# Chunk steps once in 1.5 steps, a fifth half block less in four-product form, GpSimd sums in earlier steps

## The chip, the cores and the metric

The kernel runs on one core of a Trainium2 chip. The metric is the device time of one execution, in microseconds; the figure of a version is the median over several executions. The engines are TensorE (PE; its weight loads are shown apart as PEld), VectorE (DVE), ScalarE (ACT), GpSimd (POOL) and SyncE (SP). SP issues most DMAs, ScalarE a few. Each engine works through its own instructions in order and waits where an operand is not ready.

## The reference

Two blocks, one behind the other, in float32 (the weights come as 64-bit words and are converted on the chip):

```python
# q, k, v: (4, 8, 768, 64); gamma: one number per head
for t in range(S):
    state = gamma * state + einsum('bhd,bhe->bhde', k[:, :, t], v[:, :, t])
    y[:, :, t] = scale * einsum('bhd,bhde->bhe', q[:, :, t], state)
x = y.transpose(0, 2, 1, 3).reshape(3072, 512)
h = x @ w_in                 # (512, 2048)
g = h - tanh(h)
out = g @ w_out              # (2048, 512)
```

## The kernel before

**Chunks.** The first block is computed in 24 chunks of 128 tokens. For a chunk, SP loads k, q and v (`load_chunk`, L230), GpSimd scales q and v by powers of gamma (`scale`, L248, the instruction L262), k and q are transposed, TensorE makes 64x64 products of k with v (L325) and of transposed k with transposed q (L331) in `products`, VectorE masks and accumulates the state (`mask` L335, `state` L343), TensorE forms the outputs in `outputs` and `outputs_rest` (both L379), and ScalarE puts them, transposed, into `xT` (`keep_x`, L424). Four chunks fill one `xT` tile of 512 tokens; six such tiles pass through five buffers, some of which the raw weights use at the start and one of which (`fast_x`) holds weight sums later.

From chunk 8 on the transposition is done by DMA (`turn_by_dma`, L294): ScalarE copies k and then q, split into 16-bit halves, into the tile `apart` (L300), its queue writes that to `rows` in DRAM (L303), and SP issues a transposing DMA from `rows` into `kqT` (L305) once the write has landed. There is one `apart` buffer.

**Steps.** The second block works on half blocks of 256 tokens, n = 0 to 11, and on pairs of 128 columns of w_in, m2 = 0 to 7. One (n, m2) is a step; there are 96. A step multiplies x by its two column blocks ("up", into a PSUM tile h, two buffers), forms g = h - tanh(h) on ScalarE and VectorE ("shrink"), and, two or three steps later, multiplies g by w_out ("down"). Steps 0 to 31 interleave n = 0 to 3; from step 32 on n = 4, 5, ... follow with eight steps each. Steps 0 to 7 are in an order written out by hand (L848); the rest come from the loop L925.

From n = 4 on (`FAST_UP`), the up part uses seven products in place of eight (a Strassen scheme; `fast_up`, L756), on sums of weight blocks made by GpSimd (`up_weights`, L736; one of them overwrites a block of w1) and sums of token blocks (`up_tokens`, L746). ScalarE copies the first half's products out (`up_take`, L761), GpSimd adds pairs (`up_pairs`, L766), VectorE adds them in (`up_add`, L771, L773). From n = 5 on (`FAST`), the down part uses seven products of 128x256 (`fast_products`, L647) in place of four of 128x512 (`down`, L510), on sums of w_out blocks (`fast_weights`, L588, each m2 once) and on sums of g (`fast_sums`, L598 to L601, in every step), both on GpSimd; its results are put together by VectorE after the last pair (`fast_end`, L664). The room for these sums is taken over from tiles that the chunks or the weight conversion no longer need.

**Weights.** Steps 9 to 26 also convert one block of 64-bit weights each: ScalarE (L177, L178), VectorE (L186 to L192), GpSimd (L200, L204); SP loads the block three further on, and that load waits until L190 has read the buffer.

**What sets the order around the change.** `with_chunk` (L865) says in which steps a chunk step lies: 9, 11, 13, ... 45, for chunks 5 to 23. The chunk step of chunk ci (`chunk_step`, L899) completes chunk ci, makes the products, mask and state of chunk ci+2, loads chunk ci+4, turns chunk ci+3 and makes the outputs of ci+1. So the transpose that a chunk step begins is needed by the products of the next one. At the end of the step before, GpSimd scales chunk ci+3 (L981). A chunk step stands at the start of its step, ahead of the up part; only in step `FALL` (41) it stands behind the up part's first half. In that step the lag of the down part also grows from two steps to three. `with_sums` (L873) says in which step GpSimd makes which sums.

Of the kernel before, what the change touches and what calls it, by code (L numbers as in the profile page):

```python
# [9 lines left out]
F32 = mybir.dt.float32  # L10
# [6 lines left out]
P = 128  # L17
# [14 lines left out]
def kernel(  # L32
# [27 lines left out]
    NP = H // 2  # L60
    DM = H * D
# [5 lines left out]
    NCH = NT // P  # L67
    BLK = 4
# [10 lines left out]
    xp = ctx.enter_context(tc.tile_pool(name="xp", bufs=NB - 1))  # L79
    tmp = ctx.enter_context(tc.tile_pool(name="tmp", bufs=2))  # L80
    gp = ctx.enter_context(tc.tile_pool(name="gp", bufs=4))
    op = ctx.enter_context(tc.tile_pool(name="op", bufs=4))
# [56 lines left out]
    def load_weights(i):  # L139
        if i >= NW:  # L140
            return
        dst, src = weight_ends(i)
        raw = None
        if w_out.dtype != F32:
            if EARLY <= i < EARLY + 2 * len(rooms):
                raw = rooms[(i - EARLY) // 2][:, (i - EARLY) % 2]
            else:
                raw = stage.tile([P, 2 * BANK], U32, tag="raw", name=f"raw_{i}", bufs=3)
            raws[i] = raw
        if not isinstance(src, list):  # L150
            if raw is None:
                nc.sync.dma_start(out=dst, in_=src)
            else:
                nc.sync.dma_start(out=raw, in_=src.bitcast(U32))
            return
        if raw is not None:
            dst = raw.rearrange("p (c n) -> p c n", c=NC)
        for r, k, w in src:
            nc.sync.dma_start(out=dst[r, k::2], in_=w if raw is None else w.bitcast(U32))  # L159
# [46 lines left out]
    def convert(i):  # L206
        convert_begin(i)
        convert_bits(i)
        convert_end(i, nc.gpsimd)
# [18 lines left out]
    xT = {}  # L228
# [186 lines left out]

    def keep_x(ci):
        n, nj = divmod(ci, BLK)
        if nj == 0:
            xT[n] = xp.tile([P, NP, BLK * P], F32, tag="xT", name=f"xT_{n}")

        half = xT[n][:, :, ts(nj // 2, TH)].rearrange("p (n r) t -> p r n t", r=2)
        y = y_banks[:, ci % 2][:, :: 1 - 2 * (ci % 2)]
        for odd in range(2):
            nc.scalar.copy(out=half[:, :, :, ds(P * odd + D * (nj % 2), D)],  # L424
                           in_=y[:, :, :, odd::2])
# [4 lines left out]
    sums = {}  # L430
# [81 lines left out]

    def add_up(n, m2, j):
        done = 2 * m2 + 2 == NM
        if j == 0 and n not in sums:
            sums[n] = [op.tile([P, 2, DM], F32, tag="sum", name=f"sum_{n}"), set()]
        o, begun = sums[n][0][:, j], sums[n][1]
        if j in begun:
            nc.vector.tensor_tensor(o, o_p[j], o, op=ALU.add)
        elif done and j % 2:  # L520
            nc.vector.tensor_copy(o, o_p[j])
        else:
            nc.scalar.copy(out=o, in_=o_p[j])
        begun.add(j)
        if done:
            nc.sync.dma_start(out=rows_of(n)[:, j], in_=o)

    def rows_of(n):

        return out[ds(n * TH, TH)].rearrange("(p two) c -> p two c", two=2)  # L530
# [17 lines left out]

    FAST = 5
    PAIRS = NM // 2
    t_of = {}

# [27 lines left out]
    def fast_weights(m2):  # L582

        b11, b12, b21, b22 = (w2[:, 2 * m2 + i, ts(c, TH)] for i in range(2) for c in range(2))
        t = {k: next(late_room) for k in (2, 3, 4)}
        t[1] = b12
        for k, x, y in ((3, b22, b12), (1, b12, b11), (2, b22, t[1]), (4, t[2], b21)):
            nc.gpsimd.tensor_tensor(t[k], x, y, op=ALU.subtract)  # L588
        t_of[m2] = t
# [133 lines left out]
    FAST_UP = 4  # L723
# [4 lines left out]
    def up_weights(m2):  # L728

        a11, a12, a21, a22 = (w1[:, ds(2 * c, 2), ts(2 * m2 + i, P)]  # L730
                              for i in range(2) for c in range(2))
        s_ = {k: next(up_room).rearrange("p (c m) -> p c m", c=2) for k in (2, 3, 4)}
        s_[1] = a21
        for k, x, y, how in ((3, a11, a21, ALU.subtract), (1, a21, a22, ALU.add),
                             (2, s_[1], a11, ALU.subtract), (4, a12, s_[2], ALU.subtract)):
            nc.gpsimd.tensor_tensor(s_[k], x, y, op=how)  # L736
        s_of[m2] = (a11, a12, s_[4], a22, s_[1], s_[2], s_[3])
# [13 lines left out]
    def fast_up(n, m2, some):  # L751
        if 1 in some:
            hps[n, m2] = bank("h", f"h_{n}_{m2}")
        for k in some:
            for c in range(2):
                nc.tensor.matmul(hps[n, m2][:, ts(PLACE[k], P)], s_of[m2][k - 1][:, c],  # L756
                                 x_of[n][k - 1][:, c], start=(k == 1 and c == 0), stop=(c == 1),
                                 skip_group_check=True)

    def up_take(n, m2):  # L760
        nc.scalar.copy(out=odd_room[0], in_=hps[n, m2])  # L761
# [20 lines left out]
    def downs(lag, half=None):  # L782

        while len(waiting) > lag:
            tile_ = waiting[0] if half == 0 else waiting.pop(0)
            if tile_[0] >= FAST:
                if tile_ == steps[-1]:
# [13 lines left out]
    BEGUN = 8  # L801
# [60 lines left out]


    FIRST = 8
    with_chunk = {BEGUN + 2 * i + 1: FIRST - 3 + i for i in range(NCH - FIRST + 3)}  # L865
    with_weights = {BEGUN: [12, 13]}
    for i in range(14, NW):
        with_weights[i - 5] = [i]
# [1 line left out]
    FIRST_UP = steps.index((FAST_UP, 0, True, False))  # L870
    FIRST_DOWN = steps.index((FAST, 0, True, False))
    FALL = FIRST_DOWN + 1
    with_sums = {}  # L873
    for m2 in range(PAIRS):
        with_sums.setdefault(FIRST_UP - 4 + m2, []).append(lambda m2=m2: up_weights(m2))
        with_sums.setdefault(FIRST_DOWN + m2, []).append(lambda m2=m2: fast_weights(m2))

    def first_tokens():
# [5 lines left out]
    def more_tokens(n):  # L884
        up_tokens(n, op.tile([P, 4 * TH], F32, tag="sum", name=f"x_{n}"))

    with_sums[FIRST_UP - 2].append(first_tokens)
    for n in range(FAST_UP + 1, 2 * NB):
        at_ = FIRST_UP + 3 + n - FAST_UP if n < FAST_UP + 3 else PAIRS * (n - 1) + 2
        with_sums.setdefault(at_, []).append(lambda n=n: more_tokens(n))  # L890
    before = None

# [6 lines left out]
    def chunk_step(ci):  # L899
        if ci >= FIRST:  # L900
            outputs_rest(ci)
            keep_x(ci)
        middle()
        if before:
            shrink_factors(*before)
            shrink_last_factor(*before)
        if FIRST <= ci + 2 < NCH:
            products(ci + 2)
            mask(ci + 2)
            state(ci + 2)  # L910
        load_chunk(ci + 4)
        if not before:
            turn_and_see(ci)
        elif FIRST <= ci + 1 < NCH - 1:
            outputs(ci + 1)
# [9 lines left out]
    for s in range(BEGUN, len(steps)):  # L925
        n, m2, first, last = steps[s]
        fast = n >= FAST_UP
        ci = with_chunk.get(s)

        falls_back = s == FALL  # L930
        lag = LAG + int(s >= FALL)
        if ci is not None and not falls_back:
            chunk_step(ci)
        for i in with_weights.get(s, []):
            convert(i)
            load_weights(i + 3)
        if fast:
            fast_up(n, m2, (1, 5, 7, 6))
            up_take(n, m2)
        else:  # L940
            for i in range(2):
                up(n, m2, i)
        if falls_back:
            chunk_step(ci)
        if before and ci is not None:
            turn_and_see(ci)
        if ci == NCH - 2:
            outputs(ci + 1)
            see(ci + 1)
        waiting.append(steps[s])  # L950
        if fast:
            if before and ci is None:
                shrink_factors(*before)
                shrink_last_factor(*before)
            up_pairs()
            for make in with_sums.get(s, []):
                make()
            downs(lag, 0)
            fast_up(n, m2, (2, 3, 4))
            up_add(n, m2)  # L960
            shrink_begin(n, m2)
            if before:
                shrink_end(*before)
                if before[0] >= FAST:
                    fast_sums(*before)
            downs(lag, 1)
            end_some(1)
            shrink_two(n, m2)
            before = n, m2
            if s + 1 not in with_chunk:  # L970
                middle()
        else:
            shrink_begin(n, m2)
            shrink_factors(n, m2)
            shrink_multiply(n, m2)
            downs(lag)
            shrink_last_factor(n, m2)
            shrink_end(n, m2)
            for make in with_sums.get(s, []):
                make()  # L980
        if s + 1 in with_chunk:  # L981
            for which in range(2):
                scale(with_chunk[s + 1] + 3, which, nc.gpsimd)
# [67 lines left out]
```

## Time and profile before

| | |
|---|---|
| median of four executions | 705.17 us (704.98 to 705.69) |
| the profiled execution | 705.92 us |
| its span on the core | 704.1 us |
| TensorE busy | 694.3 us |
| VectorE busy | 514.3 us |
| ScalarE busy | 432.2 us |
| GpSimd busy | 344.4 us |

The span is the time between the first and the last instruction on the core; the execution's own time has some 1.8 us around it. A row of the timeline gives start and length in microseconds, engine, line, operation, "output<-inputs" and how many like instructions are merged in it; brackets at the end give the idle time before it and what ended it. SPq and ACTq are the instructions with which SP and ScalarE issue DMAs. Matmul rows include the pipeline's latency, so neighbouring rows overlap: lengths of stretches are read from start to start.

### The profile page before, as it was taken

To read this page: it belongs to the slowest core of one execution; us is meant where nothing else is said; L and a number is where in the kernel's file an instruction comes from. 1 tells how busy PE (TensorE), PEld (TensorE's weight loads), DVE (VectorE), ACT (ScalarE), POOL (GpSimd) and SP (SyncE) were. 2 spreads that over 40 slices of the span, in tenths; PEclk is the share of its full clock that TensorE was granted. 3 is DMA by queue.
4 is the path that set the end of the run, shared out by engine and by line. 5 is a ranking of instruction groups with operands and counts; after the bars stand their busy time and mean duration, and the time that the engine had idled before them with its cause. 6 is when DMAs were issued, how large, how long until landed. Compare 5 with 4: busy or idle time off the path is not lost.

```text
span 704.1 us, 16524 instructions
## 1 busy us (share of the span) xinstructions
PE 694.3 (99%) x6554; PEld 570.6 (81%) x6554; DVE 514.3 (73%) x882; ACT 432.2 (61%) x818; POOL 344.4 (49%) x491
## 2 busy tenths in 40 slices
PE   7999999999999999999999999999999999999997
PEld 6786666666677766776789999999999999999996
DVE  3888888987888756667667776676677676776765
ACT  4667657777676655565666555556655555666553
POOL 1374444545454562576278853454453544543333
PEclk9999999999999999999999999999999999999999
DMA  8791437777666454564200000000000000000001
GB/s 220 205 276 34 134 93 208 189 201 180 182 171 159 123 165 136 136 161 110 61 32 1 1 2 16 16 1 30 1 1 32 1 1 31 2 16 16 1 16 46
DMA packets 119679, 59.97 MB, mean 85 GB/s; under 512 B 101809, under 2 KB 112689, under 8 KB 119601
## 3 DMA queue, kind: packets, MB, share of 16 engines
q1 hardware_dynamic: 117008, 50.21, 27.5%
q10 hardware_dynamic: 2592, 8.69, 3.1%
q8 instruction: 52, 0.85, 0.5%
q14 instruction: 27, 0.21, 0.1%
HBM read 35.83 MB, written 14.68 MB: 72 GB/s over the span
## 4 chain that ended last, share of the span: by engine, by line
PE 93%; SPq 2%; DVE 2%; ACT 1%; issue 1%; DMA 1%; POOL 0%; POOLq 0%; DVEq 0%; ACTq 0%
PE h L756 28%; PE o L510 19%; PE h L443 15%; PE fast_t L647 8%; PE fast_o L647 7%; PE y L647 7%; PE y L379 3%; PE s L325 1%; PE s L331 1%; PE h_early L443 1%; SPq L159 1%; SPq L240 1%; PE kqTp L276 1%; DMA raw<-in_moe_w_in_dram 1%; SPq L245 1%
## 5 line engine op out<-in xcount | busy, mean ns | idle before, releaser
L510 PE MATMUL o<-w,g 128*128 128x512 f32 x320 | 145.3, 593 | 0.0
L456 ACT ACTIVATE th<-h 128x512 f32<-128x512 f32 x64 | 38.2, 598 | 136.0 <-DVE h L773 133.5
L443 PE MATMUL h<-xT,w 128*128 128x256 f32 x480 | 110.7, 382 | 0.0
L598 POOL TENSOR_TENSOR s<-g 128x128 f32<-128x128 f32 x56 | 25.6, 458 | 164.3 <-DVE g L502 160.4
L443 PEld LDWEIGHTS h<-xT,w 128*128 128x128 f32 x480 | 89.7, 190 | 19.0 <-issue 6.9
L510 PEld LDWEIGHTS o<-w,g 128*128 128x128 f32 x320 | 59.1, 190 | 55.0 <-issue 51.9
L502 DVE COPY_PREDICATED g<-large,th 128x512 f32<-128x512 int32 x96 | 86.2, 897 | 9.4
L200 POOL TENSOR_TENSOR low<-low,power 128x512 f32<-128x512 f32 x30 | 38.7, 1290 | 105.5 <-DVE power L192 80.1
L756 PEld LDWEIGHTS h<-xT,w 128*128 128x128 f32 x512 | 76.5, 191 | 14.0 <-issue 7.2
L771 DVE TENSOR_TENSOR h<-h,fast_head 128x256 f32<-128x256 f32 x64 | 27.7, 433 | 72.6 <-PE h L756 67.5
L481 DVE TENSOR_TENSOR th<-h,th 128x512 f32<-128x512 f32 x94 | 64.1, 681 | 21.4 <-ACT th L454 20.2
L756 PE MATMUL h<-xT,w 128*128 128x128 f32 x512 | 78.6, 276 | 0.2 <-ACT fast_head L761 0.2
L462 ACT ACTIVATE q<-u,tab 128x512 f32<-128x512 f32 x96 | 69.7, 726 | 1.7
L494 DVE SCALAR_TENSOR_TENSOR g<-q,h 128x512 f32<-128x512 f32 x64 | 44.0, 688 | 34.9 <-ACT q L470 33.2
L470 ACT ACTIVATE q<-u,tab 128x512 f32<-128x512 f32 x96 | 69.4, 723 | 0.0
L766 POOL TENSOR_TENSOR fast_head<-fast_head 128x256 f32<-128x256 f32 x64 | 47.0, 734 | 45.0 <-ACT fast_head L761 45.0
L471 ACT ACTIVATE large<-u,tab 128x512 f32<-128x512 f32 x96 | 68.5, 713 | 0.0
L756 PE MATMUL h<-x,w 128*128 128x128 f32 x448 | 68.3, 275 | 0.0
L485 DVE SCALAR_TENSOR_TENSOR h<-q,h 128x512 f32<-128x512 f32 x94 | 64.9, 690 | 4.7 <-ACT q L462 4.6
L756 PEld LDWEIGHTS h<-x,w 128*128 128x128 f32 x448 | 59.0, 192 | 0.0
L761 ACT COPY fast_head<-h 128x512 f32<-128x512 f32 x64 | 37.5, 586 | 26.3 <-PE h L756 26.1
L501 DVE TENSOR_TENSOR g<-g,u 128x512 f32<-128x512 f32 x64 | 47.8, 747 | 0.0
(196 smaller groups left out, 1414.5 us busy)
## 6 DMA issues: line engine op xcount, KB each, us to landing
rows<-apart ACTq DMA_DIRECT2D x16, 512.0 KB, 4.2
k<-in_k_dram SPq DMA_DIRECT2D x24, 256.0 KB, 3.7
v<-in_v_dram SPq DMA_DIRECT2D x24, 256.0 KB, 5.1
raw<-in_moe_w_out_dram SPq DMA_DIRECT2D x12, 512.0 KB, 4.0
out_dram<-sum SPq DMA_DIRECT2D x22, 256.0 KB, 2.0
q<-in_q_dram SPq DMA_DIRECT2D x16, 256.0 KB, 4.7
raw<-in_moe_w_in_dram SPq DMA_DIRECT2D x14, 256.0 KB, 4.0
raw<-in_moe_w_in_dram SPq DMA_DIRECT2D x28, 128.0 KB, 3.8
```

Of the source, the lines that this page charges most:

```text
L443: nc.tensor.matmul(hp, w1[:, c, ts(2 * m2 + i, P)], xT[n // 2][:, c, ts(n % 2, TH)], start=(i == 0 and c == 0), stop=(c == NC - 1), skip_g ...
L462: nc.scalar.activation(q0, shrinking[n, m2][0], AF.Square, bias=bias0)
L470: nc.scalar.activation(q1, u, AF.Square, bias=bias1, scale=math.sqrt(A))
L471: nc.scalar.activation(large, u, AF.Relu, bias=bias_m)
L481: nc.vector.tensor_tensor(th, hp, th, op=ALU.subtract)
L485: nc.vector.scalar_tensor_tensor(hp, in0=shrinking[n, m2][2], scalar=C0, in1=hp, op0=ALU.add, op1=ALU.mult)
L501: nc.vector.tensor_tensor(flat, src, u, op=ALU.mult)
L502: nc.vector.copy_predicated(flat, large.bitcast(I32), th)
L510: nc.tensor.matmul(o_p[j], gT[n, m2][:, i, ts(j, P)], w2[:, 2 * m2 + i], start=(first and i == 0), stop=(last and i == 1))
L647: nc.tensor.matmul(accs[n][k], left[k - 1], right, start=first and k in (1, 6, 7, 4), stop=last, skip_group_check=True)
L756: nc.tensor.matmul(hps[n, m2][:, ts(PLACE[k], P)], s_of[m2][k - 1][:, c], x_of[n][k - 1][:, c], start=(k == 1 and c == 0), stop=(c == 1), ...
L766: nc.gpsimd.tensor_tensor(odd_room[1], first[:, :2], first[:, 3:1:-1], op=ALU.add)
```

## The change

Chunk steps are counted in half steps. `halves` holds 18, 22, 25, 28, ... 67, 70, 74: an even number is the start of step h/2, an odd one the place behind the up part of step (h-1)/2. So chunk steps 5 and 6 stay in steps 9 and 11, chunk step 7 goes from step 13 to behind the up part of step 12, and from there one follows every 1.5 steps: 8 in step 14, 9 behind the up part of 15, 10 in 17, 11 behind that of 18, ... 19 behind that of 30, 20 in 32, 21 behind the first up half of 33, 22 in 35 and 23 in 37. In the fast steps "behind the up part" is behind its first half, as it was in `FALL`.

`FAST` becomes 4: half block 4 also takes the seven-product down part. `FIRST_DOWN` is then 32 and `FALL` 33 (they were 40 and 41), and the sums of w_out blocks are made in steps 32 to 39. The sums of up weights are made in steps 25 to 31 (28 to 35 before), the last two sets both in step 31. The token sums of n = 5 move from step 36 to 31, those of n = 6 from 37 to 42. `xT_1` is taken from the pool ahead of `xT_0`, and the `sum` tiles of n = 0 to 3 in reverse order, so that later tiles take over buffers that come free earlier.

```diff
     def keep_x(ci):
         n, nj = divmod(ci, BLK)
-        if nj == 0:
-            xT[n] = xp.tile([P, NP, BLK * P], F32, tag="xT", name=f"xT_{n}")
+        if n not in xT:
+            for i in (1, 0) if n == 0 else (n,):
+                xT[i] = xp.tile([P, NP, BLK * P], F32, tag="xT", name=f"xT_{i}")
...
-        if j == 0 and n not in sums:
-            sums[n] = [op.tile([P, 2, DM], F32, tag="sum", name=f"sum_{n}"), set()]
+        if not sums:
+            for i in range(FAST - 1, -1, -1):
+                sums[i] = [op.tile([P, 2, DM], F32, tag="sum", name=f"sum_{i}"), set()]
...
-    FAST = 5
+    FAST = 4
...
     FIRST = 8
-    with_chunk = {BEGUN + 2 * i + 1: FIRST - 3 + i for i in range(NCH - FIRST + 3)}
+    LATER = NCH - FIRST
+    halves = [2 * BEGUN + 2] + [2 * BEGUN + 3 + 3 * i for i in range(1, LATER + 1)]
+    halves += [halves[-1] + 3, halves[-1] + 7]
+    with_chunk = {h // 2: FIRST - 3 + i for i, h in enumerate(halves)}
+    behind_up = {h // 2 for h in halves if h % 2}
...
     for m2 in range(PAIRS):
-        with_sums.setdefault(FIRST_UP - 4 + m2, []).append(lambda m2=m2: up_weights(m2))
+        with_sums.setdefault(min(FIRST_UP - 7 + m2, FIRST_UP - 1), []).append(lambda m2=m2: up_weights(m2))
         with_sums.setdefault(FIRST_DOWN + m2, []).append(lambda m2=m2: fast_weights(m2))
...
     for n in range(FAST_UP + 1, 2 * NB):
-        at_ = FIRST_UP + 3 + n - FAST_UP if n < FAST_UP + 3 else PAIRS * (n - 1) + 2
+        at_ = FIRST_UP - 1 if n == FAST_UP + 1 else PAIRS * (n - 1) + 2
...
-        falls_back = s == FALL
+        falls_back = s == FALL or s in behind_up
...
-        if falls_back:
+        if falls_back and ci is not None:
             chunk_step(ci)
```

## The prediction

> **What bounds the kernel now.** I read the page's busy shares and its chain first, then the PE timeline for the length of a step, then the timeline of all engines around two chunk steps, and last GpSimd's rows.
>
> ```profile
> PE 694.3 (99%) x6554; PEld 570.6 (81%) x6554; DVE 514.3 (73%) x882; ACT 432.2 (61%) x818; POOL 344.4 (49%) x491
> PEclk9999999999999999999999999999999999999999
> PE 93%; SPq 2%; DVE 2%; ACT 1%; issue 1%; DMA 1%; POOL 0%; POOLq 0%; DVEq 0%; ACTq 0%
> ```
> TensorE is the bound: 99% busy at full clock, 93% of the chain, no gap of note after 70 us. So only two things move the time: less PE work, or a new PE wait. Step lengths (first matmul of steps 40, 41 and of two later neighbours):
>
> ```profile
> 343.62 0.61 PE L756 MATMUL h<-xT,w 128*128 128x128 f32 x4
> 350.18 0.61 PE L756 MATMUL h<-xT,w 128*128 128x128 f32 x4
> ...
> 506.36 0.61 PE L756 MATMUL h<-xT,w 128*128 128x128 f32 x4
> 512.51 0.61 PE L756 MATMUL h<-xT,w 128*128 128x128 f32 x4
> ```
> Step 40 still has a four-product output part (6.56 us); the later ones have seven products (6.15 us).
>
> The transpose chain of chunk 9, begun in chunk step 6 (step 11) and used by the products of chunk step 7 (now step 13), on all engines and in the DMA view of that transpose:
>
> ```profile
> 116.88 1.05 POOL L262 TENSOR_TENSOR q<-q,tab 128x512 f32<-128x512 f32 x1
> 117.96 1.05 ACT L300 COPY apart<-q 128x1024 uint16<-128x1024 uint16 x1 [3.27 <-POOL q L262]
> 119.03 0.34 ACTq L303 DMA_DIRECT2D rows<-apart  x1
> 121.65 3.62 PE L443 MATMUL h<-xT,w 128*128 128x256 f32 x16
> 122.94 1.81 SPq L305 DMA_TRANSPOSE kqT<-rows  x1
> 125.10 3.60 PE L510 MATMUL o<-w,g 128*128 128x512 f32 x8
> 128.63 0.69 PE L325 MATMUL s<-v,k 64*64 64x64 f32 x32
> 129.29 0.69 PE L331 MATMUL s<-kqT 64*64 64x64 f32 x32
> ```
> ```profile
> kqT<-rows SPq DMA_TRANSPOSE x1, 6.3
> ```
> 122.94 + 6.3 = 129.24 us: the transpose lands just as L331 starts. L331 begins 0.66 us behind L325, against 0.47 in a settled chunk: it has already waited a little. This chain has no slack even two steps apart.
>
> A settled chunk step (9, in step 17):
>
> ```profile
> 160.65 0.46 PE L379 MATMUL y<-a,v 64*64 64x64 f32 x16
> 160.93 0.65 PE L325 MATMUL s<-v,k 64*64 64x64 f32 x32
> 161.40 0.65 PE L331 MATMUL s<-kqT 64*64 64x64 f32 x32
> 163.74 0.34 ACTq L303 DMA_DIRECT2D rows<-apart  x1
> 168.65 2.81 SPq L305 DMA_TRANSPOSE kqT<-rows  x1
> ```
> From the start C of the chunk's PE work: L331 at C+0.75, rows issued at C+3.1, landed at C+8.0, transpose landed 4.9 later at C+12.9.
>
> GpSimd when the first up-weight sums follow the scaling:
>
> ```profile
> 239.96 1.03 POOL L262 TENSOR_TENSOR q<-q,tab 128x512 f32<-128x512 f32 x1
> 240.96 1.03 POOL L262 TENSOR_TENSOR v<-v,tab 128x512 f32<-128x512 f32 x1
> 241.96 1.21 POOL L736 TENSOR_TENSOR fast_raw<-w 128x256 f32<-128x256 f32 x1
> ...
> 244.86 0.72 POOL L736 TENSOR_TENSOR fast_raw<-w,fast_raw 128x256 f32<-128x256 f32 x1
> ```
> One set of four sums takes 3.6 us, and it will stand before a scaling instead of behind it.
>
> **The change, part by part.**
>
> *Half block 4 in seven products.* Eight output parts go from 6.56 to 6.15: 8 x 0.41 = 3.3 us less PE. GpSimd gets 32 more sums of 0.46 us, 1.8 a step, beside 3.2 for the output weights and 0.7 for the pair sum: 5.7 of a 6.15 us step, the load that steps 42 to 47 carry now without a PE gap. If that cover went, a late set would hold the output products, three steps behind. The two `sum` copies of half block 4 become one copy and seven adds of 0.42 spread over six steps (2.9 us on VectorE, 71% busy from 500 on), with two stores of 256 KB as now on an SP queue that is then empty.
>
> *Chunk step 7 half a step after step 12's start.* Everything up to the transpose at 122.94 stands in the same order. But PE now comes to chunk 9's products when step 12's up part ends at 125.10; L331 would start at 125.10 + 0.09 + 0.5 = 125.7. The transpose lands at 129.24: PE waits 3.5 us, and queued behind it are outputs(8) and the output part of step 12. With the shortest landing of the settled chunks, 4.2, the wait is 1.4; with the queue no better, 3.5, which I take since the same loads stand before it. ScalarE's `see` waits with PE, so step 12's shrink starts near 131 instead of 125.5; its g is wanted in step 14, after 146, and covers that.
>
> *Chunk steps 1.5 steps apart.* Two steps with a chunk are 16.06 us (160.65 less 144.59); one half step is 3.45, so C to C is 12.6, and L331 needs the transpose at C+13.35. Rows issued at C+3.1 plus landings of 8.1 to 9.9 (chunk steps 8 to 15) end at C+11.2 to C+13.0. No wait at today's latencies, 0.3 to 2.1 in hand. DMA share: 7.2 us per chunk (0.45 of 16.1 without weights), 2.1 per weight step (0.71 x 16.07 = 11.4, less 7.2, halved); now (7.2 + 3.15)/12.6 = 0.82 against 0.71. Bounds: no effect, or latencies up in that ratio, 15% of 9.2 = 1.4 and 0.5 wait a chunk. VectorE: 14.27 of 16.07 now; chunk 1.5, a step 6.4; then 11.1 of 12.6, the same 88%. ScalarE's shrink of a step with its chunk behind the up part starts about 4 us later (copies, `see`); h's two buffers leave 6 us. SP's k, q, v loads come behind that step's weight load, which waits for VectorE's L190; k waits for L325 anyway.
>
> *Late scaling in front of the on-step chunks.* The shrink before them starts 4.0 after C instead of at once; the conversion on GpSimd starts 6.9 (no `sum` adds) or 8.4 (two adds) after the shrink's start (166.49 to 173.38; 182.55 to 190.94), takes 2.6, then q 1.05. q is ready at C+14.6 or C+16.1, that is 2.0 or 3.5 into the next chunk, where ScalarE wants it at 2.1. So chunk steps 10 and 14 send rows 1.3 late: 4.4 + 9.2 = 13.6 against 13.35, some 0.3 of wait each, doubled to 0.8 together for the busier DMA (bounds 0 and 2.6).
>
> *Up-weight sums three steps sooner.* In step 25 they stand between the conversion and the scaling for chunk 19: q is ready 3.6 later, 5.6 into chunk step 16. Rows go out at C+6.6 instead of C+3.1; weight loads are over, 8.1 to 9.9 then gives C+14.7 to C+16.5 against 13.35: PE waits 1.4 to 3.1, less if rows meet no loads (2.6 us in the run's best case, then 0). I take 1.9.
>
> *The rest.* In step 31 the last up-weight set waits for the last four-product up part (it overwrites w1), then come x_5 and the scaling for chunk 23: q is ready 3.2 into chunk step 20. The next chunk step follows after only 10.7 (chunk, a fast step, 1.78 of the next). With no load beside it the rows take 2.6 (as at 341.60) and the transpose 4.3: 4.4 + 6.9 = 11.3 against 11.45; at 9.2 it would be 2.1 late. I take 0.3. The first output sums' `apart` write waits for these rows, to 8 into the step; the pair sum behind it is wanted later. Room orders (xT, sums) cost nothing: xT_1 is last read in step 27, xT_0 in step 31, before the new readers; the stores of `sum` tiles end steps before. x_6 in step 42 adds 3.0 to 2.5 on GpSimd, under 6.15. Lag and FALL keep their shape, eight steps sooner.
>
> Sum: -3.3 + 3.5 + 0.8 + 1.9 + 0.3 + 0.2 (other chunks) = +3.4 us.
>
> By the Trainium skill (TensorE: Matmul & The Clock Gate, "Why this matters for your kernels" and "What's actually happening") a PE gap above about 3 us in mid kernel puts the clock back to half. Here the longest PE gap is 1.54 us, at 7.5 us, with the granted clock 1.00 on both sides, so no row shows it. Were it so at chunk 7, half of the page's 3.4 us window, an estimate of 1.7 us, would come on top: +5.1 instead of +3.4.
>
> **Rivals.**
> 1. *Saving kept.* Chunk 9's transpose lands in 4.2 and GpSimd runs ahead: -3.3 + 1.4 = 703.3. For it: the settled landings. Against: the 6.3 is this very transfer. The decisive point is a first wait under 1.9 us with no second one.
> 2. *A draw.* The first wait is all: -3.3 + 3.5, 705.4. Speaks for it: margins of 0.3 to 2.1 elsewhere.
> 3. *DMA becomes the pace.* At a share of 0.82 the rows and transposes take 1.4 longer, and 13 further chunk steps wait 0.5 each on top of the sum: +9.9, 715; half of it is 712.
>
> **How the numbers follow.** The profiled run took 705.92 (span 704.1), 0.75 above the median 705.17; its sum is 709.3, so the median should be 708.6. Chances: forecast 0.5, rival 1 0.1, a draw 0.2, rival 3 0.2. About 0.2%, 1.4 us, is what can be told from no change. Faster 0.10, same 0.20, slower 0.70. The range runs from near rival 1 to the lower part of rival 3: 703.8 to 713; the forecast's own is 706.6 to 711.
>
> **What would show it.** After: seven-product rows (L647) from step 35; a PE gap of about 3.5 us ahead of L331 near 126 to 129; a second of 1 to 3 us in step 27, with L300 on ScalarE waiting for POOL q in step 26; else dense PE. I am wrong if that transpose lands before 126, if PE finds gaps at every chunk, or if GpSimd's sums hold the output products of half block 4.

## The result, and the profile after

The changed kernel took 704.18 us in the median (703.05 to 707.43, 36 runs), the kernel before 705.62 beside it (704.49 to 708.49, 55 runs, the first four of which gave the 705.17 above): a ratio of 0.9980 with a 95% interval of 0.9974 to 0.9986. It is 1.4 us faster (1.0 to 1.8), 0.2%, where 3.4 us more were forecast. The profiled execution took 703.75 us (span 702.0).

Busy times, granted clock (PEclk, in 40 slices of the span; 9 is 90% or more of full speed) and chain of the page after:

```profile
PE 691.1 (98%) x6602; PEld 579.6 (83%) x6602; DVE 517.3 (74%) x888; ACT 432.8 (62%) x818; POOL 354.3 (50%) x523
PEclk9999999999999999999999999999999999999999
PE 85%; ACT 5%; POOL 3%; DVE 2%; DMA 2%; issue 2%; SPq 1%; ACTq 0%; POOLq 0%; DVEq 0%
```

TensorE is 3.2 us less busy than before and the clock is full throughout. But its share of the chain fell from 93 to 85%, and ScalarE and GpSimd now have 8% (1% before): in some places the chain now runs through their work, not TensorE's. This is a share of the chain, not of time lost; the waits themselves follow.

The steps of half block 4 on TensorE (first matmul of two neighbouring steps, and a seven-product row between them):

```profile
338.19 0.61 PE L758 MATMUL h<-xT,w 128*128 128x128 f32 x4
339.98 1.03 PE L649 MATMUL fast_t<-w,g 128*128 128x256 f32 x4
344.34 0.61 PE L758 MATMUL h<-xT,w 128*128 128x128 f32 x4
```

A step lasts 6.15 us here, against 6.56 at this place before. The seven products came as forecast.

The place of the forecast first gap, chunk step 7 behind the up part of step 12, on all engines:

```profile
117.22 1.05 ACT L300 COPY apart<-q 128x1024 uint16<-128x1024 uint16 x1 [3.28 <-POOL q L262]
118.30 0.34 ACTq L303 DMA_DIRECT2D rows<-apart  x1
121.73 2.04 SPq L305 DMA_TRANSPOSE kqT<-rows  x1
124.45 0.69 PE L325 MATMUL s<-v,k 64*64 64x64 f32 x32
126.11 0.69 PE L331 MATMUL s<-kqT 64*64 64x64 f32 x32 [0.96 <-DMA kqT<-rows]
```

And in the chain of waits of that stretch the two transfers by themselves (start, length, what):

```profile
118.30 3.42 DMA rows<-apart
121.73 4.33 DMA kqT<-rows
```

The wait is where it was forecast and for the transfer named. It is 1.2 us (L331 starts 1.66 behind L325, against 0.47 without a wait), not 3.5: the transpose landed 4.3 us after its issue, not 6.3.

The other place, chunk steps 16 and 17 (steps 26 and 27), on all engines:

```profile
243.11 1.04 POOL L262 TENSOR_TENSOR q<-q,tab 128x512 f32<-128x512 f32 x1
244.19 1.05 ACT L300 COPY apart<-q 128x1024 uint16<-128x1024 uint16 x1 [3.23 <-POOL q L262]
245.26 0.34 ACTq L303 DMA_DIRECT2D rows<-apart  x1
247.94 1.76 SPq L305 DMA_TRANSPOSE kqT<-rows  x1
251.74 0.65 PE L325 MATMUL s<-v,k 64*64 64x64 f32 x32
252.36 0.69 PE L331 MATMUL s<-kqT 64*64 64x64 f32 x32
256.24 1.04 ACT L300 COPY apart<-q 128x1024 uint16<-128x1024 uint16 x1 [2.65 <-POOL q L262]
256.99 3.62 PE L444 MATMUL h<-xT,w 128*128 128x256 f32 x16
258.64 0.59 ACT L455 ACTIVATE th<-h 128x512 f32<-128x512 f32 x1
259.27 0.69 DVE L482 TENSOR_TENSOR th<-h,th 128x512 f32<-128x512 f32 x1 [4.66 <-ACT th L455]
260.48 1.28 DVE L521 TENSOR_TENSOR sum<-o,sum 128x512 f32<-128x512 f32 x2
261.22 3.70 PE L511 MATMUL o<-w,g 128*128 128x512 f32 x8 [0.62 <-DVE sum L521]
```

ScalarE does wait 3.23 us for q, as forecast. But the late rows met no weight loads and landed within 2.7 us (245.26 to 247.94), so L331 was only 0.15 late. The price appears one chunk step on, in another queue: at 256.24 ScalarE is again held by q, its `tanh` of step 27 (L455) comes behind that copy, VectorE's shrink waits 4.66 us for it, the in-order addition of output banks (L521) stands behind the shrink, and TensorE finds no free bank for its output products. They start 4.23 us behind the up part (256.99 to 261.22), where 3.45 is usual: 0.8 us lost.

TensorE's rows, against an undisturbed spacing of 0.47 from L325 to L331, show one more small wait for a transpose, at 189.12 (0.19, chunk step 12). Together: 1.2 + 0.2 + 0.15 + 0.8 = 2.3 us of waits against 3.3 us of saving. That gives -1.0; the medians differ by 1.4, and the ratio's interval reaches down to 1.0.

### The profile page after: what moved, and what is told of

Its sections match the earlier page's. It is cut to its first block, busy times and chain, and to the rows that moved or that the text cites. A ratio compares the mean times of both kernels' runs of the same rounds, so it can differ in the third digit from the quotient of the medians.

```text
span 702.0 us, 16649 instructions
## 1 busy us (share of the span) xinstructions
PE 691.1 (98%) x6602; PEld 579.6 (83%) x6602; DVE 517.3 (74%) x888; ACT 432.8 (62%) x818; POOL 354.3 (50%) x523
## 4 chain that ended last, share of the span: by engine, by line
PE 85%; ACT 5%; POOL 3%; DVE 2%; DMA 2%; issue 2%; SPq 1%; ACTq 0%; POOLq 0%; DVEq 0%
PE h L758 28%; PE o L511 12%; PE h L444 11%; PE fast_t L649 10%; PE y L649 8%; PE fast_o L649 8%; PE y L379 3%; PE s L331 1%; PE s L325 1%; PE h_early L444 1%; ACT apart L300 1%; DMA raw<-in_moe_w_in_dram 1%; PE kqTp L276 1%; POOL low L200 1%; PE h_early L217 1%
## 5 line engine op out<-in xcount | busy, mean ns | idle before, releaser
L600 POOL TENSOR_TENSOR s<-g 128x128 f32<-128x128 f32 x64 | 29.3, 458 | 191.2 <-DVE g L503 187.3
L511 PE MATMUL o<-w,g 128*128 128x512 f32 x256 | 116.0, 596 | 0.6 <-DVE sum L521 0.6
L511 PEld LDWEIGHTS o<-w,g 128*128 128x128 f32 x256 | 47.5, 190 | 48.4 <-issue 44.2
```

Of the source, the lines that this page charges most:

```text
L511: nc.tensor.matmul(o_p[j], gT[n, m2][:, i, ts(j, P)], w2[:, 2 * m2 + i], start=(first and i == 0), stop=(last and i == 1))
```

## The experiments

Two theories stood at the start. **A**: the change saves 8 x 0.41 = 3.3 us, and gives some 2.3 of it back in two places, the transpose of chunk 9 (which lands too late) and the up-weight sums ahead of the scaling (which hold ScalarE). **Rival**: the saving is not what it seems, or the waits have another cause (the late scaling alone, the DMA pace).

### e1: the changed kernel again

No edit. 

> The changed kernel once more, as the base for the three kernels beside it. Theory A (one PE saving of 3.3 us from the seven products, partly given back by PE waits of some 2 us, of which the first, ahead of L331 near 126 us, is the largest and changes from execution to execution with the landing of chunk 9's transpose): 1.4 us under the kernel before; in this profile the first wait lies anywhere between 0.9 and 3.5 us. Theory B (the first wait is the same in each execution and the 6.3 us landing of before was a feature of that kernel): again 1.1 to 1.2 us of wait.

Measured 703.66 us (702.82 to 705.1, 11 runs; 705.08 before beside it), ratio 0.9982 (0.9974 to 0.9991). TensorE's rows:

```profile
124.10 0.69 PE L325 MATMUL s<-v,k 64*64 64x64 f32 x32
125.61 0.69 PE L331 MATMUL s<-kqT 64*64 64x64 f32 x32 [0.81 <-DMA kqT<-rows]
...
260.87 3.70 PE L511 MATMUL o<-w,g 128*128 128x512 f32 x8 [0.76 <-DVE sum L521]
```

Both waits recur near their size (1.0 and 0.9 us, from the spacing of the starts), and this transpose landed 4.2 us after its issue. They belong to the kernel, not to one execution.

### e2: half block 4 back in four products

```diff
-    FAST = 4
+    FAST = 5
...
-            for i in range(FAST - 1, -1, -1):
+            for i in range(3, -1, -1):
...
+        if n not in sums:
+            sums[n] = [op.tile([P, 2, DM], F32, tag="sum", name=f"sum_{n}"), set()]
```

> The seven-product down part of half block 4 alone is undone (FAST = 5); chunk steps and sums stay where the change put them. Theory A: eight steps are 0.41 us longer again, so 3.3 us over the changed kernel and 1.9 us over the kernel before: the moved chunk steps alone cost 1.9 us. Rival (the gain came from somewhere else, for instance from chunk steps taken out of the fast steps, and the seven products bring less): under 2 us over the changed kernel, and no slower than before.

Measured 712.17 us (711.66 to 712.78), ratio 1.0103 (1.0089 to 1.0116): 8.5 over the changed kernel. It does not isolate the seven products. `FAST` also moves `FALL` to step 41, where no chunk work is left beside it, and it moves the output-weight sums back to steps 40 to 47, while the token sums of n = 6 stay in step 42, where the change had put them. Rows of TensorE, GpSimd, VectorE and ScalarE there:

```profile
358.50 0.71 PE L760 MATMUL h<-xT,w 128*128 128x128 f32 x4 [0.73 <-ACT fast_head L765]
369.84 0.73 POOL L750 TENSOR_TENSOR x<-xT 128x256 f32<-128x256 f32 x1
374.47 0.72 POOL L770 TENSOR_TENSOR fast_head<-fast_head 128x256 f32<-128x256 f32 x1
375.23 0.43 DVE L775 TENSOR_TENSOR h<-h,fast_head 128x256 f32<-128x256 f32 x1 [4.14 <-POOL fast_head L770]
376.13 0.60 ACT L457 ACTIVATE th<-h 128x512 f32<-128x512 f32 x1 [5.67 <-DVE h L777]
378.49 0.71 PE L760 MATMUL h<-xT,w 128*128 128x128 f32 x4 [2.07 <-ACT fast_head L765]
```

and busy times with the granted clock (the column behind POOL) in two windows:

```profile
381.00:383.00 2.00, 2.00 (x7) 1.64 (x6) 1.31 (x3) 0.45 (x1) 1.92 (x3) 0.50 0.00 0
383.00:385.00 2.00, 2.00 (x18) 1.98 (x18) 1.90 (x4) 1.42 (x4) 1.84 (x3) 0.97 0.00 0
```

Two new waits for ScalarE, 0.73 and 2.07, and behind the longer one a stretch at half clock (0.57 from 379.5 to 381, 0.50 from 381 to 383): from 378.49 to the next half step 4.21 us instead of 2.63, 1.6 lost. The first wait stands in step 41 itself. The longer one comes from GpSimd: the pair sum (L770) stood behind four output-weight sums, the four token sums (L750, 369.84 to 372.75) and the sums of g, VectorE waited 4.14 us for it, ScalarE for VectorE, and ScalarE's copy for TensorE came last. With 3.3 that is 3.3 + 0.7 + 2.1 + 1.6 = 7.7 of the 8.5. So the number says little of the seven products alone; p3 and p6 take that up.

### e3: chunk 9's q scaled sooner

```diff
+        if s == 10:
+            scale(9, 0, nc.gpsimd)
         for i in with_weights.get(s, []):
             convert(i)
...
-            for which in range(2):
+            for which in range(int(s == 10), 2):
```

> Against the changed kernel only GpSimd's scaling of q for chunk 9 stands ahead of step 10's conversion instead of behind it, so rows and transpose of chunk 9 go out some 2.5 us sooner. Theory A: the PE wait ahead of L331 in chunk step 7 is gone; 1.2 us less than the changed kernel, and up to 3 us less if that wait is often longer than in its profile. Rival (the conversion that is now 1 us later holds step 12's weights or the shrink back, and a wait comes up elsewhere): no change.

Measured 703.38 us (702.85 to 704.58), ratio 0.9977 (0.9969 to 0.9986): as e1 (703.66). The rows of SP, ScalarE's queue and TensorE:

```profile
115.54 0.34 ACTq L303 DMA_DIRECT2D rows<-apart  x1
118.51 1.34 SPq L245 DMA_DIRECT2D v<-in_v_dram  x1
119.94 2.65 SPq L305 DMA_TRANSPOSE kqT<-rows  x1
122.69 2.85 SPq L159 DMA_DIRECT2D raw<-in_moe_w_in_dram  x3
125.09 0.69 PE L325 MATMUL s<-v,k 64*64 64x64 f32 x32
127.08 0.69 PE L331 MATMUL s<-kqT 64*64 64x64 f32 x32 [1.29 <-DMA kqT<-rows]
```

The rows left 2.8 us sooner than in the changed kernel and the transpose 1.8 sooner, but it landed 7.1 us after its issue, at 127.03 (this profile is of the slowest of e3's 11 executions, 704.58 us). Between 116 and 125 the same DMA engines carried the k, q and v loads and the raw weights, whose issues had slipped to beside it. The DMA share stood at 1.09 to 1.24 in each microsecond from 119 to 124, where the changed kernel has 0.13 and 0.00 from 121 to 123. So the first wait did not go when the scaling was early: by this one profile, a transfer that is issued sooner beside those loads lands later. That the loads are the cause is read from these shares; no run here takes them away.

### e4: the up-weight sums behind the scaling

```diff
             shrink_end(n, m2)
-            for make in with_sums.get(s, []):
-                make()
         if s + 1 in with_chunk:
             for which in range(2):
                 scale(with_chunk[s + 1] + 3, which, nc.gpsimd)
+        if not fast:
+            for make in with_sums.get(s, []):
+                make()
```

> Against the changed kernel, GpSimd makes the sums of steps 25 to 31 behind the scaling at the end of the same step instead of ahead of it. Theory A (ScalarE's waits of 3.2 and 2.7 us for q near 241 and 253 us push step 27's shrink back, VectorE's add of the o banks stands behind it, and PE waits 0.8 us ahead of L511 near 260 us for a free bank): these waits vanish, 0.9 us less than the changed kernel. Rival (that PE wait comes from the chunk step behind the up part itself, q early or late): ScalarE waits less, PE waits the same, no change in time.

Measured 702.79 us (701.86 to 705.17, 8 runs), ratio 0.9974 (0.9962 to 0.9986), 0.87 under e1 on the same chip. All engines at the two places shown above for the changed kernel:

```profile
239.12 1.05 POOL L262 TENSOR_TENSOR q<-q,tab 128x512 f32<-128x512 f32 x1
240.31 1.06 ACT L300 COPY apart<-q 128x1024 uint16<-128x1024 uint16 x1
...
255.98 0.69 DVE L482 TENSOR_TENSOR th<-h,th 128x512 f32<-128x512 f32 x1 [2.09 <-ACT th L455]
257.19 1.28 DVE L521 TENSOR_TENSOR sum<-o,sum 128x512 f32<-128x512 f32 x2
...
259.77 3.60 PE L511 MATMUL o<-w,g 128*128 128x512 f32 x8
```

q is ready before ScalarE wants it, ScalarE's copy waits for nothing, L521 runs 3.3 us sooner, and the wait for an output bank is gone. That settles its cause. This version is the fastest of those that leave nothing out; its interval overlaps the changed kernel's, so the 0.87 rests on the vanished wait as much as on the medians.

### p1, p2, p3: without the transposition

In these three the transposing DMA is a plain one of the same 512 KB and ScalarE copies the words in order, so k and q stay untransposed; everything else stands. p1 is the kernel before, p2 the changed one, p3 the changed one with half block 4 in four products as in e2, but `FALL` left in step 33.

```diff
-            nc.scalar.copy(out=apart[:, :, which],
-                           in_=words.rearrange("p (n two) -> p two n", two=2))
+            nc.scalar.copy(out=apart[:, which].rearrange("p two n -> p (two n)"), in_=words)
...
-        nc.sync.dma_start_transpose(
-            out=sides[ci].rearrange("p i n t -> p (i n) t").bitcast(U16),
-            in_=rows.rearrange("p two n -> (p two) n"),
+        nc.sync.dma_start(
+            out=sides[ci].rearrange("p i n t -> p (i n t)").bitcast(U16),
+            in_=rows.rearrange("p two n -> p (two n)"),
```

and in p3 besides the edit of e2:

```diff
-    FALL = FIRST_DOWN + 1
+    FALL = FIRST_UP + 1
```

> The kernel before with the transposition of k and q from chunk 8 on left out: the transfer from rows into kqT is an ordinary one of the same 512 KB, and ScalarE copies the words in order; the products run on untransposed data and the output is not the reference's. It is the base for the next two. Theory A (PE hardly waits for that transfer in the kernel before): within 0.5 us of the kernel before. Rival (the transposes hold PE up before as well): over 1 us less.

> The changed kernel with the same part left out. Theory A (the wait of 1.2 us ahead of L331 in chunk step 7 is the landing of the transpose, 4.2 us behind its issue, and an ordinary transfer lands in under 3 us): that wait is gone, the 0.8 us wait ahead of L511 near 260 us stays; 2.5 us under the base p1, where the change gained 1.4 with transposes. Rival (the DMA engines are full up to 126 us and any transfer lands as late, or the wait is not this one): the wait stays, 1.4 us under p1.

> As p2, but half block 4 takes the four-product down part again (FAST = 5), while the longer lag still begins in step 33, beside a chunk step, and not in step 41, where without a chunk step PE waited 0.7 and 2.1 us and then ran 3.4 us at half clock. Theory A (the seven products save 0.41 us in each of eight steps, and the chunk steps' new places bring no more than they cost): 3.3 us over p2. Rival (the places themselves cost several us, hidden by a larger saving): 5 us or more over p2.

| | median us | ratio to before (705.52) |
|---|---|---|
| p1 | 705.77 (704.95 to 706.89) | 1.0004 (0.9995 to 1.0013) |
| p2 | 702.98 (702.42 to 704.19) | 0.9965 (0.9952 to 0.9977) |
| p3 | 708.60 (707.95 to 708.81) | 1.0041 (1.0027 to 1.0055) |

In the kernel before, the transposition costs nothing that can be told (p1, within 0.1%): the transposes were hidden, but for the 0.2 us of chunk step 7. The change brings 2.8 us without it (p2 against p1, known to about 1.1) and 1.4 with it. TensorE's waits in p2:

```profile
PE y L378 <- ACT seen L408: 1.7, 3, 0.7
PE kqTp L217 <- DVE w L116: 1.1, 1, 1.1
PE y L378 <- ACT xT L424: 0.8, 1, 0.8
PE y L378 <- DVE state L347: 0.8, 2, 0.6
PE o L510 <- DVE sum L520: 0.7, 1, 0.7
```

No wait for `kqT` is left among them: the plain transfer of chunk 9 landed in 3.3 us, and the spacing from L324 to L330 there (L325 and L331 in the changed kernel) is 0.65, 0.2 above the usual. The one for the output bank still stands: 3.3 - 0.7 = 2.6, near the 2.8. The first wait is thus for the landing of the transposing DMA, and it is not needed for the second.

p3 spoke against theory A and for its rival: 5.6 us over p2, where the seven products should be worth 3.3. Its TensorE rows at two neighbouring steps, and the busy times of PE, PEld, DVE, ACT and POOL in just that window:

```profile
371.34 0.61 PE L759 MATMUL h<-xT,w 128*128 128x128 f32 x4
377.78 0.61 PE L759 MATMUL h<-xT,w 128*128 128x128 f32 x4
```

```profile
371.34:377.78 6.44, 6.41 (x43) 5.70 (x42) 4.32 (x7) 3.51 (x6) 6.13 (x10) 1.00 0.00 0
```

Eight steps up to 371.34 cost what was forecast: with starts 0.08 apart at 291 us, p3 is at that step 3.38 us after p2 (367.96), hence 3.3. Behind it six steps (44 to 49; the expectations below count them as 42 to 47) last 6.44 instead of 6.15, another 1.8. GpSimd has 6.13 us of work in a step of 6.44 and its rows there stand one behind the other without a wait: by this reading it sets the pace (p6 tries it). What put it behind shows in the trace: p3 has the output-weight sums in steps 40 to 47 and the token sums of n = 6 (3.3 us) in step 42, as e2 has. The pair sum comes 2.97 us after the start of step 42, but 5.84 after that of step 43, and 6.1 in the steps behind it. The kernel before made these token sums in step 37 and had chunk work beside steps 41, 43 and 45, which makes those steps longer. Which of the two differences counts for how much was not tried.

### p4, p6, p7: the two remaining causes, each taken away

p4 is p2 with the edit of e4. p6 is p3, and p7 is p2, with three of the four output-weight sums (the fourth is left out, which alters the output further):

```diff
-        for k, x, y in ((3, b22, b12), (1, b12, b11), (2, b22, t[1]), (4, t[2], b21)):
+        for k, x, y in ((3, b22, b12), (1, b12, b11), (2, b22, t[1])):
             nc.gpsimd.tensor_tensor(t[k], x, y, op=ALU.subtract)
+        t[4] = t[2]
```

> The changed kernel with the transposition left out (its output is not the reference's for that reason), and the up-weight sums of steps 25 to 31 placed behind the scaling. In p2_after_plain's profile one wait of note is left, 0.74 us ahead of the output products at 260.25 us (o <- DVE sum). Theory A (that wait comes from the sums standing ahead of the scaling, and from nothing in the transposition): the wait is gone and the time is 0.7 under p2's, about 702.3. Rival (the sums moved back hold up something of their own, the tokens of half block 4 or the up weights): a new wait near 290 to 310 us, and 703 or more.

> p3_five_regular_plain with three of the four sums of GpSimd for each pair of output weights: the fourth is left out and the third's tile is read in its place, so the output is wrong for that reason as well as for the transposition left out. In p3's profile steps 42 to 47 last 6.44 us instead of 6.15 and GpSimd is busy without a break in them. Theory A (the saving by seven products is 8 x 0.41 = 3.3, and the other 1.8 of p3's 5.6 over p2 come from GpSimd as the pace of these six steps): steps 42 to 47 go back to 6.15 and the time to 706.8, 1.8 under p3. Rival (the steps are longer for a reason of their own on TensorE): 708.6, as p3.

> p2_after_plain with the same sum left out, as the control to p6: in p2's profile the steps with these sums (35 to 41) last 6.15 us, 6.65 where chunk work lies beside them, and TensorE has no gap in them. Theory A (GpSimd is not the pace there): the same time as p2, 703.0, within 0.4. Rival (GpSimd's sums cost the changed kernel something too): 0.5 to 1.8 less, 701.2 to 702.5.

| | median us | ratio to before (705.52) |
|---|---|---|
| p4 | 702.01 (701.44 to 702.82) | 0.9946 (0.9933 to 0.9958) |
| p6 | 707.07 (705.80 to 708.47) | 1.0018 (1.0009 to 1.0028) |
| p7 | 703.55 (703.12 to 704.01) | 0.9966 (0.9954 to 0.9978) |

p4 is 0.97 under p2 (0.7 expected), and its TensorE waits no longer list the output bank. It stands 3.8 under p1 in medians (705.77 less 702.01), 4.1 by the ratios, which are known to about 1.2: with both waits taken away, the 3.3 of the saving is there, and perhaps a little more.

In p6 the same two steps start on TensorE at

```profile
371.59 0.61 PE L760 MATMUL h<-xT,w 128*128 128x128 f32 x4
377.74 0.61 PE L760 MATMUL h<-xT,w 128*128 128x128 f32 x4
```

6.15 us apart again; the time fell by 1.5 (1.8 expected). In p7 the same sum left out brought nothing (ratio 0.9966 against 0.9965, each known to 0.0012; in medians p7 is 0.6 above p2, but on another chip). So GpSimd was the pace in p3 and is not in the changed kernel, and p3's 5.6 is 3.3 and a cost of p3's own. Between p6 and p7, where GpSimd is the pace in neither, the seven products are worth 3.5.

## Why the prediction was wrong

**The saving.** Right: -3.3 from eight steps at 0.41. The profile shows 6.15 for 6.56, p6 against p7 gives 3.5. GpSimd's 5.7 us a step in these steps was rightly costed at nothing (p7), and e2 and p3 show how thin that cover is: with the token sums of n = 6 beside the output-weight sums, and 6.13 us of GpSimd work in each step after that, TensorE was slowed.

**The first wait, 3.5.** The step that failed most. Place, transfer and the waiting line were right; the term was mis-sized, because it took the landing of this one transfer in one profile (6.3) as its property. With the same loads ahead of it and the next weight loads issued 1.9 to 2.2 us behind it, as in the kernel before, it landed in 4.3, 4.2, 4.2 and 4.2 us in the profiles of the changed kernel, e1, e2 and e4, and the wait was 1.0 to 1.25. The prediction had the other end in hand (4.2 gives 1.4) and chose the dearer one "since the same loads stand before it". Whether 6.3 is a rare draw of the kernel before or belongs to it stays open; only one profile of it with transposes was had. Moving chunk step 7 half a step later, which might take this wait away, was not tried.

**Chunk steps 11 and 15, 0.8.** Measured nothing: L331 stands 0.48 and 0.50 us behind L325 there (176.57 and 226.99). The rows did go out late in chunk steps 10 and 14, but by 0.85 us, not 1.3. For chunk step 11 rows and transpose then landed in 8.1 us, the lower bound; for chunk step 15 in 9.5, just in time.

**Chunk step 17, 1.9.** The lateness of q was right (ScalarE waited 3.23 us for it). What failed is the landing taken for it, 8.1 to 9.9 for rows and transpose, from rows that shared the queue with weight loads. The late rows met none and landed in 2.7, 7.1 with the transpose, the case which the prediction named and priced at 0 and did not take. The profile before already had nearer rows: in its chunk steps 17 to 19 the rows go out 6.5 to 7.1 us after the chunk's start, and rows and transpose land 7.1 to 7.4 us later. Then a cost came that it did not name: it followed the late q to TensorE through the transpose only. It did not ask what is queued behind the wait on ScalarE's own queue. That was the shrink, then VectorE's addition, then an output bank: 0.8 us (0.9 in e1 and p2), shown by e4 and p4, where it goes when the sums stand behind the scaling.

**Chunk step 21, 0.3, and the other chunks, 0.2.** Nothing at chunk step 21 (0.48 from L325 to L331). The other chunks have the 0.2 of chunk step 12. The room orders show no wait on TensorE, as said.

**The sum.** With the measured terms it reads -3.3 + 1.2 + 0 + 0.15 + 0.8 + 0 + 0.2 = -1.0 instead of +3.4: the places of the two main waits were right, the landings were taken too long in both, and one path was missing.

**Rivals.** The first was nearest, "saving kept", at 703.3 with 0.1 of the chance; its deciding point, a first wait under 1.9 us with no second one, was met but for 0.8 us of a second. A DMA pace at every chunk did not come, though the DMA share rose even more than worked out, from 0.73 to 0.86 in 100 to 140 us and from 0.69 to 0.87 in 180 to 220: apart from chunk 9's, the transposes there still arrived with 0.2 us of wait at most (0.35, once, in e1). The range held 704.18 close to its low end; the chances did not fit.

**The clock rule.** The longest wait of the changed kernel was 1.2 us and the clock stayed at 1.00, so the rule of the Trainium skill (TensorE: Matmul & The Clock Gate, "Why this matters for your kernels") on gaps above about 3 us was not met there. In e2 a stretch at 0.50 followed a wait of 2.07 us; if that wait brought it on, the point lies lower than the page has it. Only one profile shows it; the mean granted clock of all four executions of e2 was 0.998, against 0.999 or 1.000 in e1's.

## What to carry to other kernels

The landing of one transfer in one profile may be a draw: when a forecast hangs on it, take the median of its kind and keep the outlier for the range. Where an instruction gets a new wait, follow its own engine's queue as well as its data: here the data path absorbed 3.2 us, and the `tanh` queued behind the copy paid. And when an experiment undoes one part, look in its profile for what else moved before its time is believed: two of these (e2, p3) cost more than the part itself, and in both GpSimd, with two kinds of sums in the same steps, had fallen behind.

## What the hardware showed unexpectedly

- In e2 TensorE waited 2.07 us between matmuls. From about one microsecond after it went on (378.49) it ran at a reduced granted clock, 0.57 from 379.5 to 381 us and 0.50 from 381 to 383, before it went back to 0.97 in the next two. Waits of 0.96 and 1.29 us in the changed kernel and e3 left it at 1.00.
- A transpose issued 1.8 us sooner (e3) landed 1.0 us later than in the changed kernel, 7.1 us after its issue instead of 4.3, with other loads beside it.
- A 512 KB write of rows landed in 3.4 us beside loads (118.30) and in 2.7 with fewer (245.26): how late a late transfer ends depended here on what it no longer met.
